# Queueing dense-row stores three units late and giving each batch its own x tiles, in a fused sparse-attention and mixture-of-experts kernel

## The chip, the core and the metric

The kernel runs on one core of a Trainium2 chip. The metric is the device time of one execution in microseconds. Before the change it is 258.98 us, the median of three runs (258.58 to 259.02). The profile is of one such execution; its span is 256.5 us.

## What is computed

The reference has two stages. The first is attention over chunks of 32 keys, for 4 batches, 8 heads, 768 positions and a head size of 64: for every query, an upper bound of its score with each chunk is taken from the chunk's smallest and largest keys, and only the six best chunks are attended, causally.

```python
ub = np.sum(np.maximum(q[:, :, :, None, :] * k_min[:, :, None, :, :],
                       q[:, :, :, None, :] * k_max[:, :, None, :, :]), axis=-1)
top_chunks = np.argsort(ub, axis=-1)[..., -top_k:]
mask = sel & (pos[:, None] >= pos[None, :])
attn = softmax(np.where(mask, scores, -1e9))      # written out in the reference
x = (attn @ v).transpose(0, 2, 1, 3).reshape(B * S, H * D)
```

The second is a mixture of experts over the 3072 rows of x (512 wide), with a dense layer beside it:

```python
y_dense = np.maximum(x @ w1_dense, 0.0) @ w2_dense
expert_idx = np.argmax(x @ w_gate, axis=1)
for e in range(E):                                # 8 experts
    mask = expert_idx == e
    y_moe[mask] = gate_w[mask, None] * (np.maximum(x[mask] @ w1[e], 0.0) @ w2[e])
return y_dense + y_moe
```

## The kernel before

**Attention.** A pair is two heads of one batch; there are 16 pairs, four to a batch. A pair has 11 score units (`units`, line 219): each is up to 512 columns of scores on PE (line 547), an exp on ScalarE (551), for the three units with diagonal tiles a triangle mask on GpSimd (553), and, one unit later, the product with v on PE (566). While pair p runs its units, the pair two ahead is prepared at fixed units: `prep_k` at unit 4 (transposes 481, copy 483 on ScalarE, chunk extremes on VectorE 490 to 494), `prep_q` at 5, `prep_ub` at 9, and `prep_s` of the next pair at unit 2 (534 to 538). GpSimd casts k, q and v (468, 470, 475) and SyncE loads them (90, 92), each into two tiles per name. At a pair's end VectorE divides by the sum and writes the two heads' columns of x into `xbig` (577). There are two tiles `xbig`, used by batches in turn.

**Fills.** When a batch's four pairs are done, its gate and dense work runs as fills between the score units of the next batch, at the units in `at` (415 to 423), counted over the 44 units of a batch: x is transposed (`xtr`, 257 and 258), the gate chooses an expert per row (`gate`), `ranks` (290 to 303) counts rows per expert with small matmuls and gives every row a slot, `place` scatters the rows of x with an indirect DMA from GpSimd into a DRAM table (368), and the dense layer runs in two groups of four `l1` (383, 385) and three `l2` (392, 395) steps. `l2` also queues the store of its 128 rows, as two halves, on SyncE's queue (398). All fills share one PSUM bank.

A row carries, behind its 512 columns, its gate weight (written by VectorE, 281) and its token number. The number is copied by GpSimd from a table `num` after each gate (282), since both x tiles are used by two batches.

**Experts.** After attention the rows are read back from the table in blocks of 128 (28 of at most 31 in this data), each of one expert: `fetch` (450, SyncE), transposes (`tx`, 684), the first product (`e1`, 692), transposes (701), the second product (`e2`, 709), the scaling on VectorE (712), and a scatter-add into the output from GpSimd (713). The last batch's gate, dense work and scatters are spread over the first blocks by `extra` (735 to 737). Blocks are fetched up to eight ahead (`AHEAD`) into `eg`, a pool of 14 tiles. The first 11 blocks (`N1`) hold no row of the last batch; from block 11 on, a scatter-add must follow all dense stores.

**What sets the order.** The text gives each engine's work by unit; a list scheduler then orders each engine's queue by priority, and each queue runs in order. So an instruction moved by a few units moves others on its engine too.

Of the kernel before, what the change touches and what calls it, by code (L numbers as in the profile page):

```python
# [8 lines left out]
FP = mybir.dt.float32  # L9
BF = mybir.dt.bfloat16  # L10
HF = mybir.dt.float16
# [6 lines left out]
def kernel(  # L18
# [50 lines left out]
    my = ctx.enter_context(tc.tile_pool(name="my", bufs=3))  # L69
    mg = ctx.enter_context(tc.tile_pool(name="mg", bufs=2))  # L70
    mx = ctx.enter_context(tc.tile_pool(name="mx", bufs=2))
    eg = ctx.enter_context(tc.tile_pool(name="eg", bufs=14))

    att = ExitStack()
    aload = att.enter_context(tc.tile_pool(name="aload", bufs=2))
# [79 lines left out]
    ebase = const.tile([128, 1, E], HF)  # L155
    erow = const.tile([1, E], FP)
    iob = const.tile([1, NBLK], FP)
    num = const.tile([128, NM, 1], mybir.dt.int32)
    zt = const.tile([128, XW], U16)
    used = const.tile([1, E + 1], FP)  # L160

# [2 lines left out]
    ro = const.tile([1, NBLK], mybir.dt.int32)  # L164
    zo = const.tile([1, E], mybir.dt.int32)
    nblk = const.tile([1, 1], mybir.dt.int32)
    xbig = [const.tile([128, NT, XW], HF, name=f"xbig{i}") for i in range(2)]

    def route_consts():
        for x2 in xbig:  # L170
            nc.gpsimd.memset(x2[:, :, Dm:XW], 0.0)
        nc.gpsimd.iota(iom8, pattern=[[0, NT], [1, E]], base=-E, channel_multiplier=0, allow_small_or_imprecise_dtypes=True)
        nc.gpsimd.memset(osum[:, 0], 0.0)
        nc.gpsimd.memset(eone, 1.0)
        nc.gpsimd.memset(used, 0.0)
# [72 lines left out]
    def batch_fills(b):  # L248
# [4 lines left out]
        def xtr(mi):  # L253
            def f():
                tp = ptile("tr", [128, NK, 128], HF, "tp")
                for ko in range(NK):
                    nc.tensor.transpose(tp[:, ko], xbig[b % 2][:, mi, ko * 128 : (ko + 1) * 128], ident)
                nc.vector.tensor_copy(xT[:, :, mi * 128 : (mi + 1) * 128], tp)
            return f

        def gate():
            lg = ptile("tr", [128, NT, E], FP, "lg")
            for mi in range(NT):
                for ko in range(NK):
                    nc.tensor.matmul(lg[:, mi], xT[:, ko, mi * 128 : (mi + 1) * 128], wg[:, ko],
                                     start=(ko == 0), stop=(ko == NK - 1))
            mxv = mg.tile([128, NT], FP, name="mxv")
            nc.vector.tensor_reduce(out=mxv, in_=lg, op=ALU.max, axis=mybir.AxisListType.X)
            dl = mg.tile([128, NT, E], FP, name="dl")
# [8 lines left out]
            nc.vector.tensor_tensor(ohb, iom8, mn.unsqueeze(2).to_broadcast([128, NT, E]), ALU.is_equal)  # L278
# [3 lines left out]
            nc.gpsimd.tensor_copy(xbig[b % 2][:, :, Dm + 2 : Dm + 4].bitcast(mybir.dt.int32), num[:, b * NT : (b + 1) * NT])  # L282

        keep = {}

# [81 lines left out]
        def put(t):  # L367
            sc = nc.gpsimd.indirect_dma_start(  # L368
                out=table, out_offset=bass.IndirectOffsetOnAxis(ap=keep["slot"][:, t : t + 1], axis=0),
                in_=xbig[b % 2][:, t].bitcast(U16), in_offset=None)  # L370
# [17 lines left out]
        def l2(g, i, hold):  # L388
            def f():
# [3 lines left out]
                                     start=(j == 0), stop=(j == NK - 1))  # L393
                ys = my.tile([128, Dm], FP, name="ys")
                nc.scalar.copy(ys, yp)  # L395
                m = b * NT + g * G + i
                for j in range(NJ):
                    st_ = nc.sync.dma_start(out=outv[m, j], in_=ys[64 * j : 64 * j + 64])
# [25 lines left out]
        return out_list, dense, ranks, [place(t) for t in range(NT)], at  # L424

    offs = []
    rows = []
# [27 lines left out]
    with (  # L455
# [21 lines left out]
        def prep_k(p):  # L477
# [6 lines left out]
                           pk.rearrange("d (T j p) -> d T p j", p=128, j=NJ))  # L484
            ks = ahead.tile([128, 2, NC], HF, name="ks")
            kc = kp.rearrange("d (c w) -> d c w", w=32)
            k1 = ahead.tile([128, 2, NC, 16], HF, name="k1")
            k2 = ahead.tile([128, 2, NC, 8], HF, name="k2")
            for i, op in enumerate((ALU.max, ALU.min)):
                nc.vector.tensor_tensor(k1[:, i], kc[:, :, 0:16], kc[:, :, 16:32], op)  # L490
                nc.vector.tensor_tensor(k2[:, i], k1[:, i, :, 0:8], k1[:, i, :, 8:16], op)
# [79 lines left out]
        def norm(p, g):  # L571
            b, hp = divmod(p, HP)
            opv = st[p]["op", g][:, : NT * (D + 1)].rearrange("p (t e) -> p t e", e=D + 1)
            rs = ahead.tile([128, NT, 1], FP, name="rs")
            nc.vector.reciprocal(rs, opv[:, :, D : D + 1])
            h0 = (2 * hp + g) * D
            nc.vector.tensor_tensor(xbig[b % 2][:, :, h0 : h0 + D],  # L577
                                    opv[:, :, 0:D], rs.to_broadcast([128, NT, D]), ALU.mult)

        for kind in ("tr", "h", "y", "rk"):  # L580
# [87 lines left out]
    with (  # L668
# [5 lines left out]
    ):  # L674
        cur.update(tr=(p1, "tr"), h=(p2, "h"), y=(p3, "y"), rk=(p4, "rk"))
        assert not fills
        a, d, ranks, places, _ = batch_fills(B - 1)

        wef = we.rearrange("p e j f -> p (e j f)")
        def tx(i):  # L680
# [118 lines left out]
```

## Time and profile before

| quantity | value |
|---|---|
| time, median of 3 | 258.98 us (258.58 to 259.02) |
| span of the profiled execution | 256.5 us |
| score matmuls, line 547, all forms | 384, 63.0 us, mean 262 ns |
| exp, line 551 | 176, 92.4 us, mean 593 ns |
| triangle masks, line 553 | 48, 33.2 us, mean 699 ns, 37.6 us idle before them |
| dense stores, line 398 | 48 of 128 KB, 72.7 to 212.4 us |
| table scatters, line 368 | 24, landing a median of 3.8 us after issue |
| scatter-adds, line 713 | 28, mean 1561 ns, landing a median of 5.1 us after issue |
| last matmul | starts with the group at 247.55 us |

A group of instructions shows its busy time and mean length, and the idle time of its engine just before it with what ended that. Releasers are inferred from semaphores; a wait for several is put down to the last. Busy shares are averages over stages with different limits, so they are read together with the table of busy time by stretches.

### The profile page before, as it was taken

To read this page: it belongs to the slowest core of one execution; us is meant where nothing else is said; L and a number is where in the kernel's file an instruction comes from. 1 tells how busy PE (TensorE), PEld (TensorE's weight loads), DVE (VectorE), ACT (ScalarE), POOL (GpSimd) and SP (SyncE) were. 2 spreads that over 40 slices of the span, in tenths; PEclk is the share of its full clock that TensorE was granted. 3 is DMA by queue.
4 is the path that set the end of the run, shared out by engine and by line. 5 is a ranking of instruction groups with operands and counts; after the bars stand their busy time and mean duration, and the time that the engine had idled before them with its cause. 6 is when DMAs were issued, how large, how long until landed. Compare 5 with 4: busy or idle time off the path is not lost. (4 is left out here: it accounts for less than half of the span.)

```text
span 256.5 us, 7304 instructions
## 1 busy us (share of the span) xinstructions
PE 213.9 (83%) x2547; PEld 142.2 (55%) x2547; DVE 181.2 (71%) x622; ACT 177.7 (69%) x331; POOL 161.5 (63%) x197
## 2 busy tenths in 40 slices
PE   0379787787899798899996989979999999999960
PEld 0256565575666576656664766646555555555520
DVE  6878899999968699985799997236633345455440
ACT  2689897887679888878897777964556455555430
POOL 3756988766468575867866553520787462888771
PEclk9999999999999999999999999999999999999995
DMA  7999999999749989999999894366398999688875
GB/s 181 263 265 254 209 252 235 247 224 213 199 107 225 252 204 212 202 290 171 279 230 247 140 181 125 87 169 176 98 301 133 242 277 240 113 138 107 112 105 76
DMA packets 75109, 49.89 MB, mean 195 GB/s; under 512 B 29632, under 2 KB 68160, under 8 KB 75072
## 3 DMA queue, kind: packets, MB, share of 16 engines
q1 hardware_dynamic: 59856, 30.33, 46.5%
q0 software_dynamic: 15216, 19.09, 45.4%
q8 instruction: 21, 0.34, 0.6%
q14 instruction: 16, 0.13, 0.1%
HBM read 41.66 MB, written 18.23 MB: 234 GB/s over the span
## 5 line engine op out<-in xcount | busy, mean ns | idle before, releaser
L551 ACT ACTIVATE ex<-sp 128x512 f16<-128x512 f32 (+1 forms) x176 | 92.4, 593 | 10.8 <-PE sp L547 10.6
L547 PE MATMUL sp<-rT,kT 128*128 128x128 f16 (+3 forms) x384 | 63.0, 262 | 2.4 <-ACT ex L551 0.8
L553 POOL TENSOR_SCALAR_AFFINE_SELECT ex<-ex 128x512 f16<-128x512 f16 x48 | 33.2, 699 | 37.6 <-ACT ex L551 37.5
L713 POOL DMA_INDIRECT out_dram<-yo,xg x28 | 43.7, 1561 | 20.2 <-DVE yo L712 12.1
L566 PE MATMUL op<-v,ex 128*128 128x65 f16 x672 | 48.7, 194 | 4.3 <-POOL ex L553 2.8
L566 PEld LDWEIGHTS <-ex 128*128 128x128 f16 x672 | 37.0, 98 | 17.7 <-POOL ex L553 6.2
L712 DVE TENSOR_SCALAR yo<-yp,xg 128x512 f32<-128x512 f32 x28 | 21.0, 750 | 24.9 <-PE yp L709 17.1
L368 POOL DMA_INDIRECT table<-xbig,slot x24 | 24.4, 1019 | 19.1 <-DVE nf L324 11.3
L547 PEld LDWEIGHTS <-kT 128*128 128x128 f16 x384 | 28.3, 98 | 6.7 <-issue 4.2
L703 ACT COPY ehT<-tp 128x512 f16<-128x512 f16 x28 | 16.4, 585 | 19.8 <-PE tp L701 19.8
L692 PE MATMUL hp<-we,exT 128*128 x112 | 29.1, 379 | 1.1 <-DVE xbig L577 1.1
L709 PE MATMUL yp<-we,ehT 128*128 x112 | 28.7, 379 | 0.8 <-ACT ehT L703 0.8
L383 PE MATMUL hp<-xT,wd 128*128 128x384 f16 x128 | 26.2, 325 | 1.7 <-ACT hT L385 1.1
L392 PE MATMUL yp<-wd,hT 128*128 128x512 f16 x96 | 24.4, 378 | 1.0 <-ACT ys L395 0.4
L695 ACT ACTIVATE eh<-hp 128x512 f16<-128x512 f32 x28 | 16.7, 598 | 11.5 <-PE hp L692 10.9
L395 ACT COPY ys<-yp 128x512 f32<-128x512 f32 x24 | 14.2, 593 | 10.2 <-PE yp L392 6.6
L490 DVE TENSOR_TENSOR k<-kp 128x384 f16<-128x384 f16 x32 | 13.8, 469 | 9.9 <-ACT kp L483 9.8
L385 ACT ACTIVATE hT<-hp 128x384 f16<-128x384 f32 x32 | 15.9, 496 | 6.6 <-PE hp L383 6.3
L686 DVE COPY exT<-tp 128x512 f16<-128x512 f16 x28 | 11.8, 423 | 11.5 <-PE tp L684 10.5
L483 ACT COPY kp<-pp 128x768 f16<-128x768 f16 x16 | 12.9, 804 | 7.9 <-PE pp L481 7.9
L577 DVE TENSOR_TENSOR xbig<-op,rs 128x384 f16<-128x384 f32 x32 | 17.6, 550 | 0.4
L475 POOL CAST v<-vf 128x768 f16<-128x768 f32 x16 | 13.9, 871 | 5.0 <-DMA vf<-in_v_dram 3.0
(124 smaller groups left out, 403.0 us busy)
## 6 DMA issues: line engine op xcount, KB each, us to landing
we<-in_moe_w_dram POOLq DMA_DIRECT2D x16, 512.0 KB, 8.2
kf<-in_k_dram SPq DMA_DIRECT2D x32, 192.0 KB
qf<-in_q_dram SPq DMA_DIRECT2D x32, 192.0 KB
vf<-in_v_dram SPq DMA_DIRECT2D x32, 192.0 KB
out_dram<-ys SPq DMA_DIRECT2D x48, 128.0 KB
xg<-table SPq DMA_DIRECT2D x28, 136.0 KB
table<-zt SPq DMA_DIRECT2D x9, 136.0 KB
wd<-in_moe_w_dense_dram POOLq DMA_DIRECT2D x2, 512.0 KB, 6.3
```

The lines of the kernel that those rows point to most:

```text
L368: sc = nc.gpsimd.indirect_dma_start(out=table, out_offset=bass.IndirectOffsetOnAxis(ap=keep["slot"][:, t : t + 1], axis=0), in_=xbig[b % 2 ...
L383: nc.tensor.matmul(hp, wd[:, ko, j * 128 : (j + 1) * 128], xT[:, ko, g * G * 128 : (g + 1) * G * 128], start=(ko == 0), stop=(ko == NK - 1))
L392: nc.tensor.matmul(yp, hold["h"][:, j, i * 128 : (i + 1) * 128], wd[:, NK + j], start=(j == 0), stop=(j == NK - 1))
L547: nc.tensor.matmul(sp[:, o : o + w], kT[p % NB][g][:, kt * 128 : (kt + 1) * 128], rT[p % NB][g][:, a * 128 : z * 128], start=(o == 0), sto ...
L551: nc.scalar.activation(ex[:, 0:o], sp[:, 0:o], AF.Exp, scale=-0.125)
L553: latest["pool"] = nc.gpsimd.affine_select(out=ex, in_=ex, compare_op=ALU.is_ge, fill=0.0, base=0, pattern=[[0, 4], [1, 2], [2, 64]], chan ...
L566: nc.tensor.matmul(s["op", g][:, t * (D + 1) : (t + 1) * (D + 1)], ex[:, o : o + 128], v16[p % NB][:, g, kt, :], start=first, stop=(last_o ...
L577: nc.vector.tensor_tensor(xbig[b % 2][:, :, h0 : h0 + D], opv[:, :, 0:D], rs.to_broadcast([128, NT, D]), ALU.mult)
L692: nc.tensor.matmul(hp, s["xT"][:, ko], wef[:, bass.ds(offs[i] + ko * 512, 512)], start=(ko == 0), stop=(ko == NK - 1))
L709: nc.tensor.matmul(yp, s["hT"][:, j], wef[:, bass.ds(offs[i] + (NK + j) * 512, 512)], start=(j == 0), stop=(j == NK - 1))
L712: nc.vector.tensor_scalar(o, yp, s["x"][:, Dm : Dm + 2].bitcast(FP), None, ALU.mult)
L713: sc = nc.gpsimd.indirect_dma_start(out=out, out_offset=bass.IndirectOffsetOnAxis(ap=s["x"][:, Dm + 2 : Dm + 4].bitcast(mybir.dt.int32), a ...
```

## The change

It has three parts, and two reductions of buffers that pay for the space. Dense steps of a batch now begin two units earlier (unit 8 instead of 10), and the store of a row tile is a step of its own, three units behind its `l2` (in the expert stage, one block behind), so that SyncE should not stand waiting for the rows. Every batch has an x tile of its own, so that no write has to wait for the scatters of the batch two before. With that, a token's number never changes in its place, and is written once at the start, by eight iotas on GpSimd, instead of being copied after each gate. The pool `eg` goes from 14 to 11 tiles, and the scratch tiles `k1` and `k2` from two to one.

```diff
-    eg = ctx.enter_context(tc.tile_pool(name="eg", bufs=14))
+    eg = ctx.enter_context(tc.tile_pool(name="eg", bufs=11))
...
-    num = const.tile([128, NM, 1], mybir.dt.int32)
...
-    xbig = [const.tile([128, NT, XW], HF, name=f"xbig{i}") for i in range(2)]
+    xbig = [const.tile([128, NT, XW], HF, name=f"xbig{i}") for i in range(B)]
     def route_consts():
-        for x2 in xbig:
+        for b, x2 in enumerate(xbig):
             nc.gpsimd.memset(x2[:, :, Dm:XW], 0.0)
+            for j in range(NJ):
+                nc.gpsimd.iota(x2[64 * j : 64 * j + 64, :, Dm + 2 : Dm + 4].bitcast(mybir.dt.int32)[:, :, 0],
+                               pattern=[[128, NT]], base=b * S + j, channel_multiplier=2)
...
-        for j in range(NJ):
-            nc.gpsimd.iota(num[64 * j : 64 * j + 64, :, 0], pattern=[[128, NM]], base=j, channel_multiplier=2)
...
-            nc.vector.reciprocal(xbig[b % 2][:, :, Dm : Dm + 2].bitcast(FP), ss)
-            nc.gpsimd.tensor_copy(xbig[b % 2][:, :, Dm + 2 : Dm + 4].bitcast(mybir.dt.int32), num[:, b * NT : (b + 1) * NT])
+            nc.vector.reciprocal(xbig[b][:, :, Dm : Dm + 2].bitcast(FP), ss)
...
                 nc.scalar.copy(ys, yp)
+                hold["ys", i] = ys
+            return f
+
+        def store(g, i, hold):
+            def f():
+                ys = hold["ys", i]
                 m = b * NT + g * G + i
...
+        stores = {}
...
                 dense.append(l2(g, i, hold))
+                stores[len(dense) - 1] = store(g, i, hold)
...
-            at.setdefault(10 + n * (U - 12) // len(dense), []).append(f)
+            at.setdefault(8 + n * (U - 12) // len(dense), []).append(f)
+            if n in stores:
+                at.setdefault(11 + n * (U - 12) // len(dense), []).append(stores[n])
...
-            k1 = ahead.tile([128, 2, NC, 16], HF, name="k1")
-            k2 = ahead.tile([128, 2, NC, 8], HF, name="k2")
+            k1 = ahead.tile([128, 2, NC, 16], HF, name="k1", bufs=1)
+            k2 = ahead.tile([128, 2, NC, 8], HF, name="k2", bufs=1)
...
             extra.setdefault(1 + n * (N1 - 2) // len(d), []).append(f)
+            if n in stores:
+                extra.setdefault(2 + n * (N1 - 2) // len(d), []).append(stores[n])
```

The other lines of the change put `xbig[b]` for `xbig[b % 2]`.

More of the change, by code (lines that the diff above doesn't have):

```diff
@@ L256, in f @@
                 for ko in range(NK):
-                    nc.tensor.transpose(tp[:, ko], xbig[b % 2][:, mi, ko * 128 : (ko + 1) * 128], ident)
+                    nc.tensor.transpose(tp[:, ko], xbig[b][:, mi, ko * 128 : (ko + 1) * 128], ident)
                 nc.vector.tensor_copy(xT[:, :, mi * 128 : (mi + 1) * 128], tp)
@@ L369, in put @@
                 out=table, out_offset=bass.IndirectOffsetOnAxis(ap=keep["slot"][:, t : t + 1], axis=0),
-                in_=xbig[b % 2][:, t].bitcast(U16), in_offset=None)
+                in_=xbig[b][:, t].bitcast(U16), in_offset=None)
             apart(sc, "rows", "every token has a row of its own")
@@ L422, in batch_fills @@
         for n, f in enumerate(dense):
-            at.setdefault(10 + n * (U - 12) // len(dense), []).append(f)
-        return out_list, dense, ranks, [place(t) for t in range(NT)], at
+            at.setdefault(8 + n * (U - 12) // len(dense), []).append(f)
+            if n in stores:
+                at.setdefault(11 + n * (U - 12) // len(dense), []).append(stores[n])
+        return out_list, dense, stores, ranks, [place(t) for t in range(NT)], at
     offs = []
@@ L576, in norm @@
             h0 = (2 * hp + g) * D
-            nc.vector.tensor_tensor(xbig[b % 2][:, :, h0 : h0 + D],
+            nc.vector.tensor_tensor(xbig[b][:, :, h0 : h0 + D],
                                     opv[:, :, 0:D], rs.to_broadcast([128, NT, D]), ALU.mult)
@@ L676 @@
         assert not fills
-        a, d, ranks, places, _ = batch_fills(B - 1)
+        a, d, stores, ranks, places, _ = batch_fills(B - 1)
         wef = we.rearrange("p e j f -> p (e j f)")
```

## The prediction, before the result was known

> **What bounds the kernel now.** The profile page's busy shares come first.
>
> ```profile
> PE 213.9 (83%) x2547; PEld 142.2 (55%) x2547; DVE 181.2 (71%) x622; ACT 177.7 (69%) x331; POOL 161.5 (63%) x197
> ```
>
> No engine is full on average, so the kernel has to be read by stages. The second view is the table of busy time by stretches of 10 us (its columns: stretch, length, then PE, PEld, DVE, ACT and POOL busy with counts, granted clock, DMA share, GB/s):
>
> ```profile
> 40.00:50.00 10.00, 8.03 (x126) 6.08 (x125) 9.72 (x38) 8.28 (x16) 7.08 (x12) 1.00 1.19 247
> ...
> 70.00:80.00 10.00, 9.28 (x119) 6.29 (x118) 7.12 (x28) 8.05 (x17) 7.26 (x9) 1.00 0.62 124
> ...
> 100.00:110.00 10.00, 9.32 (x153) 7.08 (x152) 9.71 (x40) 7.80 (x17) 7.16 (x9) 1.00 1.10 239
> ...
> 160.00:170.00 10.00, 9.85 (x104) 5.98 (x103) 2.26 (x6) 9.85 (x21) 5.22 (x7) 1.00 0.35 103
> ...
> 210.00:220.00 10.00, 10.00 (x78) 5.67 (x77) 5.23 (x10) 5.33 (x9) 4.68 (x3) 1.00 0.88 207
> ```
>
> Up to about 64 us (the first batch, no fills yet) VectorE is full. From 65 to 88 and from 112 to 128 it is PE and ScalarE, since the dense rows of the last batch run there. From 88 to 112 and 129 to 148 VectorE is full again, with PE close behind. From 150 to the last matmul at 248 it is PE. So a PE wait is worth its length only where PE leads. The list of waits names what the change touches (waiter, releaser: us in total, times, longest). First PE's own waits between 20 and 75 us, then between 75 and 175:
>
> ```profile
> PE rk L290 <- DVE oh L278: 1.2, 1, 1.2
> ```
> ```profile
> PE op L566 <- POOL ex L553: 1.1, 1, 1.1
> ...
> PE rk L290 <- DVE oh L278: 0.9, 2, 0.5
> ```
>
> Then GpSimd's number copy, and the store queue's own list:
>
> ```profile
> POOL xbig L282 <- DMA table<-xbig,slot: 2.5, 1, 2.5
> ```
> ```profile
> SPq L398 <- ACT ex L551: 21.1, 12, 7.4
> ```
>
> The timeline joins the 2.5 and the 1.1 (start, length, engine and instruction, idle before it and releaser):
>
> ```profile
> 88.11 0.63 DVE L490 TENSOR_TENSOR k<-kp 128x384 f16<-128x384 f16 x2 [1.98 <-ACT kp L483]
> ...
> 89.17 0.19 POOL L282 COPY xbig<-num 128x6 int32<-128x6 int32 x1 [2.53 <-DMA table<-xbig,slot]
> ...
> 90.03 0.30 PE L566 MATMUL op<-v,ex 128*128 128x65 f16 x4 [1.10 <-POOL ex L553]
> ```
>
> The copy waits for the scatters of the batch two before, which read the same tile. Behind it stands the triangle mask of an exp that was ready at 87.39 (ScalarE, 86.79 + 0.60), and PE waits 1.10 for that mask. VectorE, however, had just been released at 88.11, and from there it runs to 112 us almost without a gap.
>
> [...] the pair of L490 at 128.84 us took 1.89 us beside a GpSimd cast that began at 128.81, against 0.63 at 88.11 with GpSimd idle. So moving GpSimd work also moves VectorE time. [...]
>
> **The change part by part.**
>
> *Stores behind their rows.* SyncE no longer stands up to 7.4 us at a store. Behind those stores stand loads of k, q and v. In the waits of 70 to 170 us GpSimd's casts never wait for such a load: the timeline has kf issued at 80.27 us, into the tile that the cast of 79.41 had freed, for the cast after next at 96.61. Worth 0. Rows and stores keep three tiles; the next three rows of a batch come some 16 score units later. Also 0.
>
> *Number copies gone.* Two of the four ran at 40.74 us (0.57 together), two in the batches, one of them with the 2.53 us wait. In the new order no such copy is left. If the mask starts at 87.39, it ends near 88.06 and PE saves up to 1.10. The two casts behind it move from 89.93 to 88.06. At 89.93 they cost VectorE 0.83 for L494 and 0.89 for L498; elsewhere these take some 0.2 and 0.35, so 1.2 us. At 88.06 they would meet the L490 pair, which costs 1.89 - 0.63 = 1.3. As VectorE leads there, the gain lies between 0 and 1.1: I take 0.6.
>
> *Numbers written once.* GpSimd gets two more memsets (0.45 us for two at 34.25) and eight iotas of 64x6 instead of two of 64x24 (0.58 for two). The trace shows no iota of that shape: the least is 0.165 for 1x31 and the pitch of small ones at 35.3 us is 0.1, while the self-waits in the new order ask for about the 0.25 of L184. So between 0.8 and 2.0 us, less 0.58, plus 0.45: 0.7 to 1.9, I take 1.3. Behind them, at 37.78, stand two masks for which PE already waits 0.33 us, so all of it reaches PE. PE waits 0.83 us for VectorE's kb at 42.89, which swallows most, and the 0.57 of copies at 40.74 are refunded. Cost 0.5 (0 to 1.2).
>
> *Dense work two units earlier.* In the new order the first l1 of a batch (four matmuls, some 0.65 us of PE) stands ahead of the rank matmuls that wait 1.19, 0.42 and 0.50 us for the one-hot rows. It fits in those waits: at most 0.65 + 0.42 + 0.50 = 1.57. Against it, one more l2 (0.86 us of PE, 0.59 of ScalarE) now stands ahead of the batch's last key transposes (L481), from whose copy VectorE's full stretch starts at 88.11. In the first window this may cost 0.86 less some 0.3. In the second, PE waits of 0.42, 0.12 and 0.47 by 111.95 take the extra chunk up, so 0. In the third no such stretch follows. Gain 0.7, between -0.3 and 1.5.
>
> *Four x tiles.* Line 577 waited 0.4 us in all, so the scatters of the batch two before don't hold it: 0.
>
> *11 row tiles instead of 14.* A new, earlier wait: the fetch of block i now needs the scatter-add of block i - 11, not i - 14; queued behind it on SyncE are later fetches and the last batch's six stores. Scatter-adds land 5.1 us (median) after their start. Block 22 waits for the add of block 11:
>
> ```profile
> 218.19 1.56 POOL L713 DMA_INDIRECT out_dram<-yo,xg  x1 [4.20 <-DMA xg<-table]
> ...
> 249.64 1.55 POOL L713 DMA_INDIRECT out_dram<-yo,xg  x1 [0.51 <-DVE yo L712]
> ```
>
> It lands at 223.3; PE transposes block 22 at 232.02. The first, block 11, waits for an add that started at 182.45 and is used at 207.75; the others have more than 5 us too. The add at 218.19 waits for the last dense store (issued 211.84). That store now stands behind the fetch of block 18, before behind that of block 21, and both wait for the same add of block 7: same time. From 218.19 on, 17 adds at a pitch of 1.86 end near 249.8, so only some 1.7 us of delay would be hidden there. Cost 0.
>
> *k1 and k2 single.* VectorE writes and reads them in order: 0.
>
> *Sum:* -0.6 - 0.7 + 0.5 = -0.8 us: 258.98 - 0.8 = 258.2.
>
> **The rivals.**
>
> A (forecast, chance 0.50): part of the PE waits is really gained, 258.2. For it: both the 1.10 and the 1.19 lie close to stretches where PE leads.
>
> B (0.20): VectorE's full stretches swallow the gains, and the consts are swallowed by the kb wait: 259.0. For it: VectorE idles 0.17 us between 96 and 106. [...]
>
> C (0.25): slower. The consts cost 0.9, the extra l2 ahead of L481 delays VectorE's full stretch in both windows by 0.56 (1.1), and a gain of 0.65 comes only in the third: +1.35, and with half of the second window's delay taken up by PE's waits, +1.1: 260.1. For it: VectorE had waited 1.98 us for exactly that copy. Against: PE's waits of 0.57 at 79.50 and 84.35 just before it can take up some.
>
> D (0.05): the row tiles or the last stores hold the end: block 11's add slips by over 1.7 us, or a fetch is late, 261 or more. Against: the 4 us and more of slack worked out above.
>
> **How the numbers follow.** The time is A's, 258.2. Its bounds: best -1.1 - 1.5 + 0 = -2.6 (256.4), but the two gains share the same VectorE stretch, so 256.8 as the low end; C's spread (260.1, half a microsecond more if all consts show) gives 260.6 as the high end. Left out are A's last tenth, D and C's tail, under 0.2 together. The bound of 0.2% is 0.52 us: A falls by more in most of its span (0.46 of 0.50), B mostly counts as same (0.14, the rest split evenly, 0.03 each), C and D as slower, and A's remainder as same: faster 0.49, same 0.18, slower 0.33.
>
> **What would show it.** No GpSimd copy into xbig, and no mask late by a DMA near 88 us. The rank matmuls waiting under 0.6 us after 64 us. The last score work, now at 171.5 us, at about 170.7, with the distance from there to the end unchanged (85 us). Casts still without waits on loads. Wrong: if the first batch ends later than now by over 1 us (the consts), if the wait of L490 for kp near 88 us grows (the extra l2), or if PE waits for row tiles after 200 us.

## The result, and the profile after

The changed kernel takes **264.44 us** (median of four runs, 261.89 to 268.44) against 258.99 before: slower, by a ratio of 1.0135 (95% interval 1.0098 to 1.0172). This ratio and all below leave out executions that lie more than 1.5% above the fastest of their kernel (here 265.99 and 268.44 us, with granted clocks of 0.973 and 0.962 against 0.986 and 0.980), while the medians count every one. The run of 261.89 us was profiled. Its span is 260.1 us against 256.5, so 3.6 us have to be found.

The busy shares and the granted clock in 40 slices, from the page of the changed kernel:

```profile
PE 216.4 (83%) x2547; PEld 144.0 (55%) x2547; DVE 182.7 (70%) x622; ACT 177.6 (68%) x331; POOL 161.6 (62%) x201
...
PEclk9999997999999999999999999999999999999996
```

The shares are nearly those of before. The clock has one slice of 7, where the kernel before has none. The table by stretches has it too (columns: stretch, length, then PE, PEld, DVE, ACT and POOL busy with counts, granted clock, DMA share, GB/s):

```profile
40.00:50.00 10.00, 8.17 (x128) 6.62 (x129) 9.78 (x30) 6.39 (x13) 8.32 (x11) 0.83 1.01 203
```

Two of the waits that the change was to remove are gone: GpSimd has no number copy, and PE's rank matmuls no longer wait for the one-hot rows. Others took their place. From the list of waits, first PE between 20 and 75 us, then PE between 75 and 175 us, then SyncE's queue (us in total, times, longest):

```profile
PE op L576 <- POOL ex L563: 3.3, 5, 1.9
```
```profile
PE pp L530 <- DVE kb L504: 4.0, 4, 1.4
...
PE rk L290 <- ACT hT L385: 1.0, 2, 0.5
```
```profile
SPq L404 <- ACT ex L561: 13.5, 9, 6.9
SPq L404 <- ACT ys L395: 10.5, 3, 6.1
```

SyncE still stands at the stores: 28.5 us over all releasers, against 25.2 before. As then, no GpSimd cast after the first 20 us waits for a load queued behind them.

To place the loss I take the start of the first transpose of `fl` in each of the 16 head pairs from PE's timeline; it is one fixed point per head pair, and the differences are head-pair lengths.

| stretch | before, us | after, us | difference |
|---|---|---|---|
| start to head pair 3 | 37.68 | 37.98 | +0.30 |
| head pair 3 to 4 (called "head pair 4" below) | 9.27 | 10.99 | **+1.72** |
| 4 to 7 (first window of dense work) | 27.25 | 27.80 | +0.55 |
| 7 to 11 (second window) | 40.76 | 40.81 | +0.05 |
| 11 to 15 (third window) | 43.15 | 42.29 | -0.86 |
| 15 to the first expert matmul (173.05, 174.53) | 14.94 | 14.66 | -0.28 |
| from there to the end | 83.45 | 85.57 | **+2.1** |

**Head pair 4.** GpSimd's timeline of the changed kernel (start, length, instruction) ends its constants and then does what had been queued behind them:

```profile
36.59 0.33 POOL L173 IOTA xbig<- 64x6 int32 x2
...
37.42 0.33 POOL L173 IOTA xbig<- 64x6 int32 x2
...
39.97 1.31 POOL L563 TENSOR_SCALAR_AFFINE_SELECT ex<-ex 128x512 f16<-128x512 f16 x2
41.23 0.97 POOL L478 CAST k<-kf 128x768 f16<-128x768 f32 x1
42.15 0.95 POOL L480 CAST q<-qf 128x768 f16<-128x768 f32 x1
```

In the kernel before the same three stood at 37.78, 39.03 and 39.97, so everything is 2.2 us later; 0.3 of it was there before head pair 3. The mask in GpSimd's timeline before:

```profile
37.78 1.31 POOL L553 TENSOR_SCALAR_AFFINE_SELECT ex<-ex 128x512 f16<-128x512 f16 x2
```

PE waits for the mask. VectorE's work on `k` waits for no mask, and starts 0.3 us earlier than before. VectorE's timeline before, and then after:

```profile
40.62 0.65 DVE L490 TENSOR_TENSOR k<-kp 128x384 f16<-128x384 f16 x2
41.19 0.88 DVE L491 TENSOR_TENSOR k<-k 128x192 f16<-128x192 f16 x2
...
42.63 0.21 DVE L494 TENSOR_TENSOR kb<-ks,hmask 128x96 f16<-128x96 f16 x1
```
```profile
40.31 2.11 DVE L500 TENSOR_TENSOR k<-kp 128x384 f16<-128x384 f16 x2
42.34 1.04 DVE L501 TENSOR_TENSOR k<-k 128x192 f16<-128x192 f16 x2
...
43.94 0.21 DVE L504 TENSOR_TENSOR kb<-ks,hmask 128x96 f16<-128x96 f16 x1
```

The same two pairs of instructions took 1.5 us and now take 3.15, because the masks and the casts of k and q slid onto them: the first pair ends at 42.42, 0.2 us after the cast of k. So `kb`, for which PE waited 0.83 us before, comes 1.3 us later as well. In this trace that costs PE nothing. PE's timeline has the mask wait, and after it a first use of `kb` at 44.94 instead of 42.89, without any wait, since `kb` had been ready at 44.15:

```profile
40.71 0.30 PE L576 MATMUL op<-v,ex 128*128 128x65 f16 x4 [1.90 <-POOL ex L563]
...
44.94 0.21 PE L530 MATMUL pp<-kb,qp 128*128 128x48 f16 x2
```

Between the two PE was hardly idle, but right after the mask wait its clock is at half for some 3.4 us (table by stretches of 2 us):

```profile
40.00:42.00 2.00, 0.96 (x17) 0.84 (x18) 1.97 (x3) 0.00 (x0) 2.00 (x3) 0.76 0.77 158
42.00:44.00 2.00, 2.00 (x21) 1.63 (x19) 2.00 (x7) 1.24 (x3) 1.68 (x3) 0.50 1.20 196
44.00:46.00 2.00, 1.85 (x35) 1.41 (x33) 1.99 (x6) 1.92 (x4) 1.35 (x3) 0.88 1.05 288
```

The same table with head pair 4 as one stretch, before and after, parts the loss:

```profile
37.68:46.95 9.27, 7.01 (x119) 5.37 (x117) 8.95 (x31) 7.72 (x16) 8.01 (x14) 1.00 1.17 238
```
```profile
37.98:48.97 10.99, 7.97 (x119) 6.24 (x118) 10.67 (x31) 7.82 (x16) 9.56 (x19) 0.84 1.02 220
```

PE runs the same 119 matmuls, 0.96 us longer at the lower clock, and is idle for 3.02 us instead of 2.26. In the idle time the mask's wait is 1.57 us longer (1.90 against 0.33) and the 0.83 for `kb` is gone. Of the 1.72 us, then, 0.76 is waiting, and 0.96 is longer running, for which the trace shows no other reason than the clock.

**The second window.** The mask near 88 us is no longer late, but the gain is missing from the table (+0.05). VectorE's line that answers to the 0.63 at 88.11 is now as long as two casts:

```profile
90.28 1.90 DVE L500 TENSOR_TENSOR k<-kp 128x384 f16<-128x384 f16 x2 [1.89 <-ACT kp L493]
```

Here the later `kb` does reach PE: it waits 1.41 us for it at 93.67, where before it had waited 1.10 us for the mask at 90.03.

**The expert stage.** ScalarE waits for a free `ys` tile, and PE for ScalarE (timelines of ScalarE and of PE):

```profile
205.30 0.59 ACT L395 COPY ys<-yp 128x512 f32<-128x512 f32 x1 [2.41 <-DMA out_dram<-ys]
207.68 0.58 ACT L395 COPY ys<-yp 128x512 f32<-128x512 f32 x1 [1.80 <-DMA out_dram<-ys]
```
```profile
205.94 1.02 PE L719 MATMUL yp<-we,ehT 128*128 x4 [1.79 <-ACT ys L395]
```

The first store of the last batch starts at 199.07 us, 3.75 later than before (195.32), since it now lies behind the fetches of blocks 11 and 12. The scatter-add of block 11 (timeline of GpSimd) starts 1 us later than before, and waits less; the last one is 3.7 us later, behind PE, whose last matmul moved by as much (247.55 to 251.21):

```profile
219.17 1.56 POOL L723 DMA_INDIRECT out_dram<-yo,xg  x1 [1.80 <-DVE exT L696]
...
253.30 1.55 POOL L723 DMA_INDIRECT out_dram<-yo,xg  x1 [0.52 <-DVE yo L722]
```

So a first reading had three parts: constants +1.9, earlier dense work -1, late last stores +2.2. The experiments left only the first of the three standing, and added a fourth, VectorE's two-input operations on `k` that meet GpSimd's work.

### The profile page after: what moved, and what is told of

It is laid out like the page before. It is cut to its first block, busy times and chain, and to the rows that moved or that the text cites. A ratio compares the mean times of both kernels' runs of the same rounds, so it can differ in the third digit from the quotient of the medians.

```text
span 260.1 us, 7308 instructions
## 1 busy us (share of the span) xinstructions
PE 216.4 (83%) x2547; PEld 144.0 (55%) x2547; DVE 182.7 (70%) x622; ACT 177.6 (68%) x331; POOL 161.6 (62%) x201
## 5 line engine op out<-in xcount | busy, mean ns | idle before, releaser
L557 PE MATMUL sp<-rT,kT 128*128 128x128 f16 (+3 forms) x384 | 63.8, 265 | 2.3 <-ACT ex L561 0.8
L500 DVE TENSOR_TENSOR k<-kp 128x384 f16<-128x384 f16 x32 | 17.6, 586 | 8.2 <-ACT kp L493 8.1
L530 PE MATMUL pp<-kb,qp 128*128 128x48 f16 x192 | 11.3, 187 | 8.9 <-DVE kb L504 8.7
```

The costliest lines, as they stand in the source:

```text
L557: nc.tensor.matmul(sp[:, o : o + w], kT[p % NB][g][:, kt * 128 : (kt + 1) * 128], rT[p % NB][g][:, a * 128 : z * 128], start=(o == 0), sto ...
```

## Experiments

Each of the four sets ran on one chip of its own, and the kernel before took from 258.7 to 264.9 us on them. So a variant is compared with the kernel before, or with another variant, of its own set.

### First set: the parts alone

The changed kernel again.

> The changed kernel once more, to see how far its runs lie apart and which of them have a low PE clock. Theory 'three parts': two losses that are in every run (about 1.9 us behind the number writes at 37 to 40 us, about 2.2 us behind a late store near 205 us) and a gain of about 1.0 us at the end of attention, so its best runs are near 262 (ratio 1.011). Rival 'clock': the loss is mostly the granted PE clock, which was 0.50 from 42 to 44 us in the profile after; then runs with a mean clock of 0.989, as before the change, are within 1 us of the kernel before, and the slow ones have a lower clock.

The tiles and the numbers of the changed kernel, with the old order of dense work and stores:

```diff
-            at.setdefault(8 + n * (U - 12) // len(dense), []).append(f)
+            at.setdefault(10 + n * (U - 12) // len(dense), []).append(f)
             if n in stores:
-                at.setdefault(11 + n * (U - 12) // len(dense), []).append(stores[n])
+                at.setdefault(10 + n * (U - 12) // len(dense), []).append(stores[n])
...
-                extra.setdefault(2 + n * (N1 - 2) // len(d), []).append(stores[n])
+                extra.setdefault(1 + n * (N1 - 2) // len(d), []).append(stores[n])
```

> The kernel before with the four x tiles and the numbers written once (and the 11 row tiles and single scratch tiles that pay for them); dense steps and stores at their old places. Theory 'three parts': the triangle masks near 38 us start about 1.7 to 2.0 us late and nothing takes it up: +1.7 to +2.0 us, the end of the first batch (first rank matmul) at 66.3 to 66.7 instead of 64.6, and no late store: 260.8. Rival 'row tiles': 11 tiles cost in the expert blocks, so the stretch from the end of attention to the end of the kernel grows by 2 us as well and the time is 262 to 263. My prediction's step: +0.5 with the copies' gain of 0.6 inside it, 258.9.

The kernel before with the new order in attention only (`8 +` for the dense work, `11 +` for the stores):

> The kernel before with two x tiles and its number copies; only the dense steps of batches 0 to 2 two units earlier and their stores three units behind. Theory 'three parts': the gain of the last window alone, -1.0: 258.0, the end of attention at about 170.5 instead of 171.5, first batch unchanged at 64.6. Rival: the gain came from the missing copies, so no gain here: 258.8 to 259.2.

The kernel before with the last batch's stores one block later only (`2 +`):

> The kernel before, with only the last batch's six stores put one block later in the expert stage (14 row tiles, two x tiles). Theory 'three parts': the first of these stores comes behind two row fetches, the fourth dense row waits longer for its tile, PE gets a gap near 203 us of 1.5 to 2 us: +1 to +2.2, 260 to 261.2. Rival 'row tiles': with 14 tiles the fetches ahead of the store don't wait, so no loss: 259.0.

| kernel | median us (runs) | ratio to before (95%) | mean clock |
|---|---|---|---|
| before | 263.24 (39) | | 0.988 |
| changed, again | 265.13 (20) | 1.0064 (1.0037 to 1.0090) | 0.980 |
| tiles and numbers alone | 266.70 (4) | 1.0106 (1.0042 to 1.0171) | 0.984 |
| order in attention alone | 266.26 (4) | 1.0115 (1.0025 to 1.0205) | 0.984 |
| late last stores alone | 263.22 (20) | 1.0009 (0.9983 to 1.0036) | 0.989 |

Late stores alone cost nothing that can be measured: that part of the first reading falls. The order alone, foreseen as a gain by the prediction, loses, though by little in two of its four runs (264.45, 264.48, 268.05 and 268.20 us). The rival of the clock stays open here: no run of the changed kernel has a clock of 0.989, so none could show its time at that clock. The tiles alone lose 1.06%, somewhat more than the 1.7 to 2.0 us that I had expected of the constants, and the trace shows head pair 4 at 12.29 us, worse than in the first trace of the changed kernel. VectorE's timeline there, and then PE's:

```profile
40.35 2.11 DVE L500 TENSOR_TENSOR k<-kp 128x384 f16<-128x384 f16 x2
42.38 2.44 DVE L501 TENSOR_TENSOR k<-k 128x192 f16<-128x192 f16 x2
...
45.38 0.21 DVE L504 TENSOR_TENSOR kb<-ks,hmask 128x96 f16<-128x96 f16 x1
```
```profile
45.64 0.21 PE L530 MATMUL pp<-kb,qp 128*128 128x48 f16 x2 [1.85 <-DVE kb L504]
```

Here both pairs stand, `kb` is 2.75 us later than in the first trace of the kernel before (2.4 counted from the start of head pair 4), and PE waits 1.85 us for it, besides 1.91 for the mask. The changed kernel's second trace has the same 2.12 and 2.44, and 12.28 us. In the trace of the order alone such groups take 2.52 us at 78.11 and 1.21 and 1.67 at 89.05 and 90.19; PE's waits for `kb` behind them are 1.78 and 1.99 us, and a half-clock stretch follows the second. After the first 20 us its waits for `kb` sum to 6.1 us there; in the trace of the late last stores alone they sum to 2.5.

### Second set: the numbers out of the way

If GpSimd's constants are the cause, they only have to stand elsewhere. At its start GpSimd waits 2.66 us for the first k. The clearing of the four tiles and the eight iotas move there:

```diff
+    xbig = [const.tile([128, NT, XW], HF, name=f"xbig{i}") for i in range(B)]
+    for b, x2 in enumerate(xbig):
+        nc.gpsimd.memset(x2[:, :, Dm:XW], 0.0)
+        for j in range(NJ):
+            nc.gpsimd.iota(...)
     for i in range(NB):
         nc.vector.memset(kT[i][0][64:128], 0.0)
...
     def route_consts():
-        for b, x2 in enumerate(xbig):
-            nc.gpsimd.memset(x2[:, :, Dm:XW], 0.0)
-            for j in range(NJ):
-                nc.gpsimd.iota(...)
```

The kernel before once more, for its trace; the changed kernel with this edit; the tiles alone (old order) with it; and the changed kernel with it and with the last stores at `1 +`:

> The kernel before, unchanged, for its trace on the same chip as the next three. All theories: within 0.5% of its own median; attention ends (first expert matmul of the last batch's stage) near 174.5 us, as in the run with only late tail stores, against 173.05 in the first trace; two-input minimum and maximum operations on VectorE sum to about 26 us, PE waits for kb to about 6 us.

> The changed kernel with the eight number writes and the four tile clearings moved to the start of GpSimd's queue, where it waits 2.66 us for the first k. Theory 'GpSimd's number work at the head-pair boundary costs most of it' (its own 1.9 us, and VectorE's two-input operations on k then run beside GpSimd's casts and wait for them): head pair 4 takes 9.3 us again instead of 11.0 to 12.3, the first rank matmul comes near 65 us, the mean clock is back near 0.988, and the time is 2.5 to 3.5 us under the changed kernel, so 0.6 to 1.6 us under the kernel before (ratio 0.994 to 0.998). Rival 'the order of the dense work and the stores costs it': time stays 1.5 to 2.5 us over the kernel before. Rival 'clock falls for another reason': clock stays near 0.980.

> The kernel before with four x tiles, the numbers written at the start of GpSimd's queue, no number copies, 11 row tiles and single k1, k2, but with the old order of dense work and stores. Prediction's step 'the copies and their late mask are worth 0.6': 0.6 us under the kernel before (0.9977). Theory 'the copies were worth nothing, because VectorE's kb holds the same place': within 0.3 us of it. Rival 'row tiles or single k tiles cost': 0.8 us or more over it, with waits of fetches on row tiles after 175 us.

> As num_first, and the last batch's stores directly behind their rows as in the kernel before. Theory 'late tail stores cost nothing lasting' (they measured 1.0009 alone): same time as num_first within 0.5 us. Rival 'late tail stores cost 1.8 to 2.2 us once they lie behind the fetches of blocks 11 and 12', as the first trace suggested: 1.5 us or more under num_first.

| kernel | median us (runs) | ratio to before (95%) | head pair 4 in the trace |
|---|---|---|---|
| before | 264.94 (36) | | 9.29 |
| changed, numbers first | 268.34 (22) | 1.0109 (1.0079 to 1.0139) | 9.63 |
| tiles alone, numbers first | 268.44 (13) | 1.0129 (1.0097 to 1.0162) | 9.62 |
| numbers first, last stores early | 269.05 (4) | 1.0140 (1.0076 to 1.0204) | 9.63 |

A miss of mine, and the most useful one. Head pair 4 came back to 9.6 us as foreseen, and the kernel was still slower than before by over 1%. The new order can't be what all three have in common, since the tiles alone, with the old one, lose as much. In the trace of the changed kernel with the numbers first, head pair 8 takes 12.73 us instead of 10.15 (trace of the kernel before in this set). VectorE's, GpSimd's and PE's timelines of that place:

```profile
80.61 2.52 DVE L501 TENSOR_TENSOR k<-k 128x192 f16<-128x192 f16 x2
```
```profile
81.31 0.84 POOL L478 CAST k<-kf 128x768 f16<-128x768 f32 x1
82.08 0.93 POOL L480 CAST q<-qf 128x768 f16<-128x768 f32 x1
```
```profile
84.72 0.21 PE L530 MATMUL pp<-kb,qp 128*128 128x48 f16 x2 [1.77 <-DVE kb L504]
```

A pair that takes 0.42 us undisturbed takes 2.52, until 83.13; the second cast ends at 83.01. PE then waits 1.77 us, and its clock halves from 84 to 88. So a shift of GpSimd against VectorE can cost elsewhere what it saves at head pair 4. This is one place in one execution, though, which took 270.99 us, 2.7 over its kernel's median; the profiled executions of the two other variants (268.03 and 267.48 us) take 10.31 and 9.97 us for head pair 8, and PE's waits for `kb` after the first 20 us sum to 2.5 us in the tiles alone and to 5.1 in the other, against 2.5 in the kernel before. What the tiles alone lose isn't explained by them.

What has grown in the trace with the long pair shows in its groups (mean ns of one behind the busy time). The first two, with two inputs, had 491 and 404 in the kernel before on this chip, and the third 338:

```profile
L500 DVE TENSOR_TENSOR k<-kp 128x384 f16<-128x384 f16 x32 | 16.5, 552 | 8.4 <-ACT kp L493 8.3
L501 DVE TENSOR_TENSOR k<-k 128x192 f16<-128x192 f16 x32 | 13.8, 466 | 0.0
L502 DVE TENSOR_REDUCE ks<-k 128x24 f16<-128x192 f16 x32 | 9.7, 338 | 0.0
```

Single ones of the first two range from 0.34 and 0.24 to over 1.7 us, those of the third only from 0.33 to 0.35. The third meets GpSimd's work as well: in the first traces of the two kernels 12 and 19 of its 32 reductions overlap a cast or a mask, and all of them take 0.33 to 0.35 us.

### Third set: the same work as reductions alone

The tree of two two-input operations and a reduction gives way to one reduction of all 768 elements. The result is the same maximum and minimum:

```diff
-            k1 = ahead.tile([128, 2, NC, 16], HF, name="k1", bufs=1)
-            k2 = ahead.tile([128, 2, NC, 8], HF, name="k2", bufs=1)
             for i, op in enumerate((ALU.max, ALU.min)):
-                nc.vector.tensor_tensor(k1[:, i], kc[:, :, 0:16], kc[:, :, 16:32], op)
-                nc.vector.tensor_tensor(k2[:, i], k1[:, i, :, 0:8], k1[:, i, :, 8:16], op)
-                nc.vector.tensor_reduce(out=ks[:, i], in_=k2[:, i], op=op, axis=mybir.AxisListType.X)
+                nc.vector.tensor_reduce(out=ks[:, i], in_=kc, op=op, axis=mybir.AxisListType.X)
```

The changed kernel for comparison, and the edit in the changed kernel, in the kernel before, and in the changed kernel with the numbers first:

> The changed kernel, unchanged, beside the next three on one chip. All theories: ratio to the kernel before 1.004 to 1.015; head pair 4 (from the 4th to the 5th group of transposes of fl) takes 11.0 to 12.3 us against 9.3 before.

> The changed kernel with VectorE's tree on k (two two-input operations and a reduction of 192 elements, for the maximum and for the minimum) replaced by one reduction of 768 elements each; GpSimd's work and the order are unchanged. Estimate from the trace: a reduction of 192 takes 0.33 us, so 768 take some 0.9, two of them 1.85 against 1.7 for an undisturbed tree; the trees of the changed kernel took 2.5 each in the mean, since their two-input operations stand beside GpSimd's casts for up to 2.4. Theory 'these operations wait for GpSimd': no operation on k over 1.0 us, head pair 4 at 10.4 us or less, PE's waits for kb down from 8.7-11.6 to 6 us or less, time 1 to 2.5 us under the changed kernel on the same chip. Rival 'only GpSimd's own 1.9 us in front of the mask counts': head pair 4 stays at 11 us or more and the time moves by -0.2 to +1.0 us.

> The same replacement in the kernel before. Theory 'these operations wait for GpSimd': its trees took 2.2 us in the mean with single ones of up to 2.4, so a gain as well, but a smaller one, 0.3 to 1.5 us under the kernel before. Rival: 0.2 us more on VectorE in each head pair, time 0 to 1 us over the kernel before.

> The changed kernel with both edits: numbers at the start of GpSimd's queue and the reductions in place of the tree. Theory 'waits for GpSimd are what scatters the variants': head pair 4 at 9.7 us or less, no start over 14.5 us, and the time at or under that of the kernel before (ratio 0.990 to 1.000), where numbers first alone gave 1.0109. Rival 'the change has a cost of its own in the attention order or in the expert stage': 2 us or more over the kernel before, as numbers first alone.

| kernel | median us (runs) | ratio to before (95%) | head pair 4 in the trace |
|---|---|---|---|
| before | 258.72 (23) | | |
| changed | 266.34 (4; 263.69 to 268.37) | no interval | 10.83 |
| changed, reductions | 258.46 (12) | 0.9982 (0.9951 to 1.0014) | 11.36 |
| before, reductions | 259.14 (12) | 1.0005 (0.9974 to 1.0036) | 8.23 |
| changed, reductions, numbers first | **254.14** (4) | **0.9822 (0.9785 to 0.9860)** | 8.19 |

The group of the new form, from the last kernel's trace:

```profile
L498 DVE TENSOR_REDUCE ks<-kp 128x24 f16<-128x768 f16 x32 | 29.3, 947 | 8.2 <-ACT kp L493 8.0
```

From the start of its first operation to the end of its last, an undisturbed tree (maximum and minimum) takes 1.49 us, and two reductions take 1.81. So undisturbed the edit makes VectorE a little slower. In place it stays short: all 32 reductions lie between 0.93 and 0.95 us, and 15 of them overlap a cast. The 16 trees of a run take 1.47 to 3.77 us each, 34.3 in all, in the first trace of the kernel before, and 39.4 in all in that of the changed kernel; the reductions take 30.1.

With that alone the changed kernel is about 6 us faster than it was on the same chip and level with the kernel before. (264.35 is the mean of the two runs of the changed kernel that a ratio would count, 258.38 the median of ten with reductions; there is no interval.) PE's list of waits after the first 20 us shows the change, first for the changed kernel on this chip, then with reductions:

```profile
PE pp L530 <- DVE kb L504: 4.9, 6, 1.4
```
```profile
PE pp L526 <- DVE kb L500: 0.7, 3, 0.3
```

With the numbers first as well the kernel is 1.8% under the kernel before. In it PE's wait for `kb` near 80 us is 0.16 us. The edit does two other things. It shifts the order elsewhere: head pair 2 takes 9.1 us instead of 7.7 and head pair 6 takes 11.7 instead of 10.7 in every trace with reductions. And it takes away the single tiles `k1` and `k2`; that these held VectorE isn't seen, since VectorE sat idle for 0.0 us before L501 and L502 above, and before L500 for `kp`, but it was not tried apart.

Two expectations missed. Head pair 4 stayed at 11.36 us in the changed kernel with reductions, where I had put 10.4 at most: GpSimd's own delay (PE waits 2.34 us for the mask there) and a stretch of half clock from 41 to 47 us fill it. Head pair 4 with the constants at their place, and then with the numbers first:

```profile
37.94:49.30 11.36, 8.68 (x109) 6.94 (x108) 8.24 (x26) 7.10 (x14) 8.63 (x21) 0.70 0.82 162
```
```profile
37.70:45.89 8.19, 6.41 (x108) 4.81 (x107) 7.96 (x25) 6.49 (x13) 5.41 (x8) 1.00 1.09 236
```

Of the 3.17 us between them, 2.27 are PE running longer at the lower clock and 0.90 are waiting. So the rival was right for that place: without any late `kb`, GpSimd's delay and the clock behind it cost it all, and with the numbers away the time falls by a further 4.3 us (258.46 to 254.14). And the kernel before gained nothing from the reductions, where I had put 0.3 to 1.5, although PE's waits for `kb` after the first 20 us fell to 1.0 us in it. Part of the reason is in its trace, where the number copies still stand. GpSimd's and PE's timelines:

```profile
92.59 0.19 POOL L282 COPY xbig<-num 128x6 int32<-128x6 int32 x1 [3.58 <-DMA table<-xbig,slot]
```
```profile
93.59 0.30 PE L562 MATMUL op<-v,ex 128*128 128x65 f16 x4 [2.29 <-POOL ex L549]
```

The copy's wait had grown from 2.53 to 3.58 us, and PE's for the mask behind it from 1.10 to 2.29. The head pair around them takes 11.02 us, and 9.25 in the changed kernel with reductions and the numbers first, which has no copy.

### Fourth set: which part carries the gain

> Numbers first and reductions in place of the tree, as before, on the chip of the next three. Theory 'the gain is lasting': ratio to the kernel before 0.978 to 0.988. Rival 'it was one chip's luck in a kernel of many small waits': 0.99 or more.

> As flat_first_again, but with the old order: dense work at unit 10 instead of 8, stores directly behind their rows, in attention and in the last batch. Theory 'the earlier dense work carries most': 2 to 4 us over flat_first_again. Rival 'the tiles without copies and the reductions carry it, the order nothing': within 0.8 us of flat_first_again. The prediction gave the order 0.7 us and the copies 0.6.

> As flat_first_again, with the last batch's stores directly behind their rows. Theory 'late tail stores cost nothing lasting' (alone they measured 1.0009, 0.9983 to 1.0036): within 0.6 us of flat_first_again. Rival 'they hold the ys tiles behind two fetches, as the first trace of the changed kernel shows': 1 to 2 us under flat_first_again.

The last is the kernel before with one number changed:

```diff
-    eg = ctx.enter_context(tc.tile_pool(name="eg", bufs=14))
+    eg = ctx.enter_context(tc.tile_pool(name="eg", bufs=11))
```

> The kernel before with 11 row tiles instead of 14 and nothing else. Prediction's step: 0, since the fetches have more slack; within 0.3% of the kernel before. Rival 'fetches come too late': 1 us or more, with PE waits on exT after 200 us.

| kernel | median us (runs) | ratio to before (95%) |
|---|---|---|
| before | 259.42 (27) | |
| changed, reductions, numbers first | 255.67 (6) | 0.9866 (0.9824 to 0.9909) |
| the same with the old order | 255.50 (6) | 0.9855 (0.9810 to 0.9900) |
| the same with the last stores early | 255.35 (6) | 0.9864 (0.9822 to 0.9906) |
| before with 11 row tiles | 259.07 (20) | 1.0002 (0.9979 to 1.0026) |

The gain holds on a second chip, at 1.3%. The order of dense work and stores is worth nothing within about 1 us either way, and so are the late last stores (in the traces the distance from the first expert matmul to the end is 85.1 us with late and 84.1 with early stores, one trace each). The profiled execution with the old order has a disturbance of its own: a cast of v waits 4.51 us for its load at 141.13, and PE waits 3.62 us behind it. The row tiles cost nothing. What is left for the gain is the x tiles and what came with them: by elimination, they are worth about 1.5% (kernel before with reductions 1.0005, on the third chip, against 0.9855 for the tiles in the old order, on the fourth), provided the numbers don't stand in front of a mask. The old constants can't be it: with them head pair 4 takes 8.23 us, without 8.19. That it is the missing number copies and their masks, and not the tiles' freedom itself, is argued from the one place above (11.02 against 9.25 us) and was not tried apart.

## Why the prediction was wrong, step by step

The forecast was 258.2 us; the time lies over the whole range (256.8 to 260.6).

- **Numbers written once, cost 0.5.** This is the step that failed, and head pair 4 lost 1.7 us in the first trace and 3.0 in two later ones. The delay was 1.9 us (the 2.2 of the mask without the 0.3 from before), the top of its range of 0.7 to 1.9, where 1.3 was taken. PE's clock was put at nothing: behind the mask wait it halved, which made PE run 0.96 us longer. And the clause "PE waits 0.83 us for VectorE's kb at 42.89, which swallows most" took `kb` as fixed. In the first trace the 0.83 was indeed swallowed, but only because PE itself had become slow: `kb` had moved by 1.3 us. In the traces of the tiles alone and of the changed kernel again it moved by 2.4 us, counted from the start of head pair 4, since the delayed casts met VectorE's two-input operations, and PE's wait for it grew to 1.85 and 1.86. The prediction had this in hand ("moving GpSimd work also moves VectorE time", with its 1.89 against 0.63) and charged it to the copies, but not to the constants.
- **Number copies gone, gain 0.6.** The working was right: it said that the L490 pair near 88 would then cost 1.3 us more, and it does (1.90 against 0.63). In the changed kernel that leaves nothing visible, where 0.6 was taken. Without the two-input operations the tiles without copies are worth about 1.5% by the elimination above, so what the removal is worth depends on what stands beside it.
- **Dense work two units earlier, gain 0.7.** In the first pair of traces the third window gained 0.86 and the first lost 0.55, with 0.05 in the second. Alone it cost 1.15% (0.25 to 2.05), and its trace has 3.6 us more of PE's waits for `kb` than that of the late stores alone; with these away it is worth 0 within some 1 us. So a gain of 0.7 is not seen anywhere as one of its own.
- **Stores behind their rows, 0.** Only attention was thought of. In the expert stage a new wait did appear (the 2.41 and 1.80 us above). But the kernel before already had one of 1.88 us there, and measured alone the later stores cost 0 (1.0009). Right in size as far as the medians tell, with a wait overlooked.
- **11 row tiles, 0.** Right (1.0002). **Four x tiles and single k1, k2, 0:** never measured apart from the numbers. Nothing in the traces speaks against it, but what the tiles lose with the tree in place is not all explained.
- **Rivals.** C, "slower, consts 0.9 and the extra l2 1.1", named the right side and the first of its causes, at 0.9 where 1.7 was measured. Its second is not seen: the wait of `k` for `kp` near 88 us went from 1.98 to 1.89, not up. So its side is in part luck. The sign set beforehand, a first batch ending over 1 us later, came true: `fl` of head pair 6 stands at 67.33 instead of 65.30.

**What stays open.** Of the 3.6 us of the first pair of traces, the 2.1 of the expert stage are not settled. In the first set that distance is 85.6 us for the changed kernel and 87.5 for late stores alone, where PE never waits for a row copy. But such a wait comes back in the third set's trace of the changed kernel (2.06 us at 208.42, with a half-clock stretch behind it; 86.5 us to the end), and smaller ones of 0.79 to 1.27 stand in the traces of the reductions with late stores, against 0.59 and none in the two with early ones. The medians with late and with early stores don't show a difference. And the variants with the numbers first but the tree in place lose more than their traces explain. "Numbers first, last stores early" has trees of only 36.8 us (their groups' busy time) against 35.9 in the kernel before, and is 1.4% slower; the tiles alone with the numbers first wait no longer for `kb` than the kernel before, and are 1.3% slower. The trace of the former shows ScalarE idle for 2.06 us before the row copy at 160.24 and VectorE for 1.56 at 75.12, with releasers that had long been done. Such stalls, some of them marked "issue", stand in the kernel before on these chips too (2.37 us at 115.19). I didn't find their cause.

## What to carry to other kernels

Work added to an engine's queue is not priced by its length and the slack behind it alone: ask which instructions of other engines it now runs beside, and what PE's clock does behind a new wait (here about 3.4 us at half behind 1.90 us of waiting). Where VectorE's operations grow beside GpSimd's casts, another form of the same work can cost more undisturbed and less in place: here two reductions took 1.81 us against the 1.49 of an undisturbed tree, but 30.1 us over a run against 34.3 and 39.4 of the trees in the kernel before and the changed one. As long as such collisions are in a kernel, the gain or loss of a reordering can be no more than their new alignment, as with the earlier dense work here (a ratio of 1.0115 with them, nothing beyond some 1 us without). When a removed wait brings nothing, look first for the instruction that became longer.

## What the runs showed of the hardware that was not expected

VectorE's two-input operations on `k`, where they were long, ended just behind a GpSimd instruction. In the first traces of the two kernels, 15 and 20 of the 64 such operations on `k` took over 0.08 us longer than undisturbed, and every one of them ended 0.10 to 0.27 us after the end of a cast, a mask or (twice) an indirect DMA. Which one it ends behind differs: at head pair 4 of the changed kernel, three operations in a row end behind three GpSimd instructions in a row, while in the trace of the tiles alone a single one, of 0.25 us undisturbed, takes 2.27, through a cast, a mask and another cast. Two inputs are not the whole of it: in each of the two first traces 9 of the 32 copies from `kp` to `kT`, which read one tile, took 0.44 to 0.89 us, where most take 0.31 to 0.37, and they ended 0.16 to 0.21 us behind the end of a GpSimd instruction.

PE's clock halved behind waits that were mostly shorter than the stretch that followed. In the changed kernel a wait of 1.90 us is followed by about 3.4 us at half clock (the lines at 40 to 46 us). Between start-up and the end, the 18 traces have 16 such stretches, of 3.4 us each but for one of 6.85; each begins within 2 us of the end of a PE wait of 1.4 to 3.6 us. A wait of this kind doesn't always do it: in the first trace of the changed kernel the clock stays at 1.00 behind waits of 1.41 us before 93.67 and before 134.47, and of 1.79 us before 205.94. What a stretch costs can be read from one and the same kernel on two chips (changed, reductions, numbers first; table by stretches, third set, then fourth):

```profile
30.00:34.00 4.00, 3.22 (x51) 2.58 (x52) 3.37 (x7) 2.76 (x5) 1.71 (x3) 1.00 1.18 189
```
```profile
30.00:34.00 4.00, 3.58 (x40) 3.47 (x41) 2.84 (x6) 1.54 (x3) 0.83 (x2) 0.57 1.19 188
```

PE waits 2.40 us before 30.32 in the one and 2.39 before 30.42 in the other. In the first the clock holds and head pair 3 takes 7.38 us, in the second it halves and the head pair takes 8.55: 1.2 us for one such stretch. In 20 runs of the changed kernel the mean clock is 0.980, in 39 of the kernel before 0.988, which by estimate would be a little over one more such stretch in a run (0.5 x 3.4 of 264 us is 0.0064); the three traces of the changed kernel have one, one and three, those of the kernel before none.
